# Four weight sums on GpSimd moved behind one transfer, in a transformer block on one core

## The chip, the core and the metric

The kernel runs on one core of a Trainium2 chip. The core has a matrix engine (TensorE, PE in the profile), three element-wise engines (VectorE or DVE, ScalarE or ACT, GpSimd or POOL), a synchronising engine that issues transfers (SyncE, SP), and sixteen DMA engines. Every engine takes its own instructions in the order in which they were written; between engines, semaphores order the work. The metric is device time in microseconds of one execution: 1111.73 us is the median of three runs of the kernel before (1110.59 to 1112.41).

## What is computed

A parallel block: a layer norm of x (2048 rows of 576), then x + attention + a feed-forward part, both taken from the same normed rows. The attention is local and dilated: 32 heads of 18, each position looks at 8 keys, 2 apart.

```python
def _A_ref(x, wqkv, wo):
    H = 32; Dh = D // H
    W, dil = 8, 2
    qkv = ... (x @ wqkv).reshape(B, S, 3, H, Dh) ...
    idx = pos[:, None] - off[None, :]            # off = arange(W) * dil
    logits = einsum("bhsd,bhswd->bhsw", q, k[idx]) * scale, masked where idx < 0
    o = einsum("bhsw,bhswd->bhsd", softmax(logits), v[idx])
    return o @ wo
def _B_ref(x, w1, w2):                           # w1: 576 x 4608, w2: 4608 x 576
    return maximum(x @ w1, 0) @ w2
x = A_x
xn = _layernorm(x)
return x + _A_ref(xn, A_wqkv, A_wo) + _B_ref(xn, B_w1, B_w2)
```

All data is float32.

## The kernel before

**Split numbers.** A float32 operand is split in two: a high part, which ScalarE writes as a rounded copy, and a low part, the rest, which VectorE or GpSimd gets by a subtraction (function `two`: L172 the copy, L176 the subtraction on VectorE, L174 the same on GpSimd where a call asks for `pooled`). A product is then three matmuls: high by high, high by low, low by high. Relu outputs are split in the same way: L793 is ScalarE's high part, L797 VectorE's low part.

**Tiling.** The 2048 rows are taken in two phases of 1024, each phase in four blocks of 256 columns after a transpose (`xT`, in SBUF). W1's 36 column tiles of 128 are taken first six by the plain way, and the other 30 in 15 pairs. A pair's product with two row blocks is a 2 by 2 block product over the first 512 of the 576 input features, done with seven products instead of eight (M1 to M7). For this the quarters A11, A12, A21, A22 of a pair of W1 are combined: S1 = A21 + A22, S2 = S1 - A11, S4 = A12 - S2, S3 = A11 - A21. `sw_load` brings the quarters into the staging tile `st` (DMAs from SyncE), `sw_mix(k)` makes one of the four combinations in `st` (L958, one GpSimd instruction on 128 x 256), and `sw_prep` splits quarters and combinations into the matmul operands in `ar` (L172 and L176). Each of these operands has one place, so a split for the next pair can only follow the last matmul that reads the old one.

**Groups and steps.** A pair p has an even group 2p (row blocks 0 and 1) and an odd group 2p + 1 (row blocks 2 and 3): 30 groups a phase. `group` runs a group in eight steps. A step is a half of the seven products (two runs of twelve matmuls on the two halves of TensorE's rows, banks `ph` and `pm`), followed by a half of the second weight's product for an earlier group (`po`, columns 0 to 255 or 256 to 575). The products share four accumulators: `a` and `q` (two `ph` banks, used in turn) and `f` and `r` (two `pm` banks, in turn). In step 2 ScalarE copies `a` into a new `q` bank, and in step 5 it copies `q` into a new `r` bank (`seed`, L1026). A bank is free again when its relu or its addition has read it. So the low part (L797) of the relu read from `pm` in step 4 frees the bank of the seed in step 5, which TensorE uses in step 7, and the L797 read from `ph` in step 6 frees the bank of `a` in step 1 of the next group. The relus of steps 1 and 2 read SBUF tiles `m` and `u` (L1035 completes them on VectorE).

**The output.** When the two column parts of a row block are complete in PSUM, ScalarE copies them into a buffer `ev` (L746, one copy of 512 and one of 640 numbers for each partition), and GpSimd issues a transfer that adds the buffer to the output in DRAM (L752). There are two such buffers, and two transfers a group: one issued in step 3, one in step 7.

**Who sets the order.** `plan_strassen` writes by `on(phase, group, step, "T" or "O", ...)` what is issued in which step: "T" behind the step's first products, "O" behind its second-weight half. Beside that a queue of attention work for VectorE (`bg`: L575 products of queries and keys, L578 their sums, L587 to L602 the softmax, L610 and L617 the weighted values, L626 and L633 transposes) is drained by `run_bg`, which at fixed points of each step issues as much as a running account of VectorE's time (`t["dve"]`, raised by every `dve(n)`) leaves room for. In three stretches of a phase steps also hold the splits of a slice of the attention weights (`wq`), and two groups later 26 or 28 matmuls for queries, keys and values (L142) behind four steps of a group.

A tensor's staging is also read by `w2_split` (the second weight; 256 and 320 columns, L172 and L176, on GpSimd L174 in even groups).

Of the kernel before, what the change touches and what calls it, by code (L numbers as in the profile page):

```python
# [70 lines left out]
def tile_body(ctx: ExitStack, tc: tile.TileContext, x, wqkv, wo, w1, w2, out):  # L71
# [1010 lines left out]
    def on(ph, g, i, z, f, *a):  # L1082
        evs[ph, g, i, z].append((f, a))
# [5 lines left out]
    def plan_strassen(ph):  # L1089
        for p in range(NP):  # L1090
            a = 2 * p
            f = NC0 * C + 2 * p
            if p:
                on(ph, a - 2, 4, "O", sw_load, ph, p)
                on(ph, a - 2, 8, "O", sw_mix, 0)
                on(ph, a - 1, 1, "O", sw_mix, 1)
                on(ph, a - 1, 2, "O", sw_mix, 2)
                on(ph, a - 1, 4, "O", sw_mix, 3)
                on(ph, a - 1, 4, "T", sw_prep, ph, p, "A11")
                on(ph, a - 1, 5, "O", sw_prep, ph, p, "S2")  # L1100
                on(ph, a - 1, 7, "T", sw_prep, ph, p, "S1", "A12")
                on(ph, a, 2, "O", sw_prep, ph, p, "S3", "S4")
                on(ph, a, 3, "T", sw_prep, ph, p, "A22", "rem")
                on(ph, a - 1, 5, "O", w2_load, ph, f)
                on(ph, a - 1, 6, "O", w2_load, ph, f + 1)
                on(ph, a, 6, "T", w2_split, ph, f, (0,), True)
                on(ph, a, 8, "T", w2_split, ph, f, (1,), True)
                on(ph, a + 1, 1, "O", w2_split, ph, f + 1, (0,))
                on(ph, a + 1, 3, "O", w2_split, ph, f + 1, (1,))
        for u in range(1, NU):  # L1110
            g = QKV_G[u]
            on(ph, g - 3, 4, "O", wq_load, ph, u)
            for kt, (d, i) in enumerate(((-2, 4), (-2, 7), (-1, 1), (-1, 4), (-1, 6))):
                on(ph, g + d, i, "O", wq_split, ph, u, kt)
            for tb in range(NTB):
                a, i = g + tb // 2, 3 + 4 * (tb % 2)
                ins[ph, a, i].append((qkv_half, (ph, u, tb, False, True)))
                ins[ph, a, i + 1].append((qkv_half, (ph, u, tb, True, True)))
            on(ph, g + 2, 1, "T", halos, ph, u)
            on(ph, g + 2, 1, "T", attention, ph, u)  # L1120
            on(ph, g + 2, 4, "T", attention_rest, ph, u)
        g = QKV_G[NU - 1] + 2
        on(ph, g, 1, "O", wo_first, ph)
        on(ph, g + 1, 5, "O", wo_split, ph, 0)
        on(ph, g + 3, 3, "O", wo_split, ph, 1)
        on(ph, g + 5, 3, "O", wo_split, ph, 2)
        on(ph, NG - 1, 5, "O", hold.__setitem__, ("xs", ph), True)
        if ph == 0:
            for i in range(2):
                on(ph, NG - 1, 4 + i, "O", xt_in, 1, i)  # L1130
            for i in range(2):
                on(ph, NG - 1, 8, "O" if i else "T", xt_parts, 1, i, 0)
                on(ph, NG - 1, 8, "O", xt_parts, 1, i, 1)
            on(ph, NG - 1, 5, "O", hold.__setitem__, ("go", 0), True)
            on(ph, NG - 2, 4, "O", w1_load, 1, 0)
            on(ph, NG - 1, 5, "O", w2_load, 1, 0)
            on(ph, NG - 1, 7, "O", w2_load, 1, 1)
            on(ph, NG - 1, 6, "O", w1_split, 1, 0, 0, True)
            on(ph, NG - 1, 8, "T", w1_split, 1, 0, 1)
# [291 lines left out]
    for ph in range(NPH):  # L1431
# [65 lines left out]
        late(b + 22, sw_prep, ph, 0, "S3", "S4")  # L1497
        late(b + 23, sw_prep, ph, 0, "A22", "rem")
        plan_strassen(ph)
    ot_plan(0)  # L1500
    ot_plan(1)
# [156 lines left out]
```

## Time and profile before

| what | value |
|---|---|
| median of the runs | 1111.73 us (1110.59 to 1112.41, three runs) |
| the profiled execution | 1111.74 us, span 1109.9 us |
| TensorE busy | 1098.9 us, 99% |
| VectorE busy | 849.0 us, 76% |
| ScalarE busy | 573.5 us, 52% |
| GpSimd busy | 357.9 us, 32% |
| sums of W1 quarters, L958 | 120 of 0.952 us |
| adding transfers, L752 | 128, on GpSimd's queue |

A row of the page's table of groups names the line, the engine, the operation, out<-in by the program's names, and how many; then busy us and mean ns of one, then the idle time of the engine before them and what ended it. A row of the waits reads: who waited for whom, us in total, times, longest. A row of the timeline has the start in us from the start of the span, the duration, engine, line, operation and tiles, and in brackets the idle time of the engine before it with what ended it. Operations that follow each other on an engine can overlap by some 0.07 us.

### The profile page before, as it was taken

The numbers are of one execution on the slowest core, as the hardware profiler recorded it, in microseconds if no ns is written. First come the engines' busy times: TensorE is split into PE (matmuls) and PEld (weight loads), VectorE is DVE, ScalarE is ACT, GpSimd is POOL, SyncE is SP. The second block draws the span as 40 slices with busy tenths as digits, with TensorE's granted clock in tenths as the row PEclk, the third lists the DMA queues.
The fourth block names the chain that finished last, engine by engine and source line by source line (L and its number), as shares of the span: only waits on it lengthen the run. The fifth ranks groups of instructions, "written<-read, shape, count | busy, mean of one in ns | idle before, by whom it ended". The sixth has DMA issues, their size and how long they took to land.

```text
span 1109.9 us, 37930 instructions
## 1 busy us (share of the span) xinstructions
PE 1098.9 (99%) x16410; PEld 1087.7 (98%) x16410; DVE 849.0 (76%) x1262; ACT 573.5 (52%) x1350; POOL 357.9 (32%) x377
## 2 busy tenths in 40 slices
PE   9999999999999999999999999999999999999998
PEld 8999999999999999999999999999999999999998
DVE  7676898898897889994326349987988978989751
ACT  5443564564455365666535346635635644566560
POOL 2313441343333234433211233313413333333421
PEclk9999999999999999999999999999999999999999
DMA  8369995696596598889958258749957965988896
GB/s 244 126 161 228 194 185 100 148 200 105 125 220 131 89 221 159 152 154 261 260 88 173 37 130 165 143 76 203 186 95 153 195 109 126 210 148 159 165 220 145
DMA packets 136598, 177.26 MB, mean 160 GB/s; under 512 B 27872, under 2 KB 83936, under 8 KB 136400
## 3 DMA queue, kind: packets, MB, share of 16 engines
q0 software_dynamic: 37632, 81.40, 47.0%
q1 hardware_dynamic: 98080, 92.55, 28.7%
q8 instruction: 129, 2.11, 0.7%
q10 hardware_dynamic: 720, 0.89, 0.2%
q14 instruction: 37, 0.30, 0.1%
HBM read 74.07 MB, written 96.22 MB: 153 GB/s over the span
## 4 chain that ended last, share of the span: by engine, by line
PE 86%; DMA 6%; DVE 3%; issue 2%; ACT 2%; SPq 1%; POOL 0%; DVEq 0%; ACTq 0%; POOLq 0%
PE po L163 28%; PE po L142 21%; PE ph L163 14%; PE pm L163 11%; PE pm L142 5%; PE ph L142 4%; DMA xT<-words 2%; PE ph L130 1%; PE po L130 1%; DMA out<-ev 1%; DMA st<-in_w 1%; DVE ar L797 1%; DVE ar L176 1%; DMA att<-od 1%; DMA od<-att 1%
## 5 line engine op out<-in xcount | busy, mean ns | idle before, releaser
L163 PE MATMUL po<-ar 64*128 64x320 f32 (+1 forms) x5760 | 455.7, 290 | 1.3 <-ACT pr L746 0.9
L163 PEld LDWEIGHTS po<-ar 64*128 64x128 f32 x5760 | 397.4, 184 | 3.2 <-ACT pr L746 1.3
L163 PE MATMUL ph<-xT,ar 64*128 64x256 f32 x2520 | 318.3, 275 | 1.1 <-DVE ar L797 0.5
L752 POOL DMA_DIRECT2D out<-ev x128 | 152.5, 1191 | 477.9 <-ACT ev L746 363.4
L163 PEld LDWEIGHTS ph<-xT,ar 64*128 64x128 f32 x2520 | 285.7, 185 | 2.4 <-ACT pm L1026 1.5
L163 PE MATMUL pm<-xS,ar 64*128 64x256 f32 x2160 | 258.0, 275 | 1.8 <-ACT u L1030 1.3
L746 ACT ACTIVATE ev<-po 128x512 f32<-128x512 f32 (+1 forms) x266 | 171.9, 652 | 137.5 <-PE po L163 74.5
L163 PEld LDWEIGHTS pm<-xS,ar 64*128 64x128 f32 x2160 | 236.1, 185 | 3.0 <-ACT u L1030 2.3
L176 DVE TENSOR_TENSOR ar<-st,ar 128x256 fp32r<-128x256 f32 (+3 forms) x236 | 157.3, 680 | 69.2 <-ACT ar L172 69.0
L172 ACT ACTIVATE ar<-st 128x256 fp32r<-128x256 f32 (+3 forms) x304 | 148.6, 503 | 3.1 <-DMA st<-in_w 1.9
L142 PE MATMUL po<-wq,xT 64*128 64x432 f32 x1296 | 133.8, 353 | 0.2 <-ACT ev L746 0.2
L142 PEld LDWEIGHTS po<-wq,xT 64*128 64x128 f32 x1296 | 120.4, 185 | 2.5 <-ACT ev L746 0.4
L174 POOL TENSOR_TENSOR ar<-st,ar 128x256 fp32r<-128x256 f32 (+1 forms) x68 | 74.5, 1098 | 132.8 <-ACT ar L172 129.9
L958 POOL TENSOR_TENSOR st<-st 128x256 f32<-128x256 f32 x120 | 113.7, 952 | 6.5 <-DMA st<-in_w 2.1
L163 PE MATMUL ph<-xS,ar 64*128 64x256 f32 x720 | 102.0, 275 | 0.1
L163 PEld LDWEIGHTS ph<-xS,ar 64*128 64x128 f32 x720 | 94.3, 185 | 0.4 <-ACT ph L1026 0.3
L610 DVE TENSOR_TENSOR pr<-att 128x1152 f32<-128x1152 f32 x64 | 88.1, 1392 | 0.4
L575 DVE TENSOR_TENSOR pr<-att 128x1152 f32<-128x1152 f32 x64 | 87.8, 1383 | 0.1
L578 DVE TENSOR_REDUCE att<-pr 128x64 f32<-128x1152 f32 x64 | 85.5, 1342 | 0.1
L142 PE MATMUL po<-ar 64*128 64x256 f32 (+1 forms) x984 | 72.7, 290 | 0.1
L617 DVE TENSOR_TENSOR pr<-pr 128x1152 f32<-128x1152 f32 x64 | 70.0, 1094 | 1.4
L797 DVE SCALAR_TENSOR_TENSOR ar<-ph,ar 128x256 fp32r<-128x256 f32 x96 | 39.0, 418 | 40.0 <-ACT ar L793 39.5
(120 smaller groups left out, 1365.1 us busy)
## 6 DMA issues: line engine op xcount, KB each, us to landing
out<-ev POOLq DMA_DIRECT2D x128, 576.0 KB, 7.3
st<-in_w SPq DMA_DIRECT2D x72, 288.0 KB, 5.6
st<-in_w SPq DMA_DIRECT2D x63, 256.0 KB, 3.6
att<-att SPq DMA_DIRECT2D x16, 441.0 KB, 4.5
att<-in_wqkv SPq DMA_DIRECT2D x28, 216.0 KB, 6.3
od<-att SPq DMA_DIRECT2D x32, 160.0 KB, 5.8
att<-in_x SPq DMA_DIRECT2D x14, 288.0 KB, 4.0
st<-in_w SPq DMA_DIRECT2D x60, 64.0 KB, 6.4
```

Source lines behind the costliest of these rows:

```text
L142: ins = nc.tensor.matmul(o, l[z], r[z], start=start, stop=stop)
L163: b.ins = nc.tensor.matmul(b.ap, l[part], r[part], start=start, stop=stop, skip_group_check=skip)
L172: nc.scalar.activation(hi, src, AF.Copy)
L174: nc.gpsimd.tensor_tensor(lo, src, f32(hi), op=ALU.subtract)
L176: nc.vector.tensor_tensor(lo, src, f32(hi), op=ALU.subtract)
L575: nc.vector.tensor_tensor(pr[i], q, window(k, i), op=ALU.mult)
L578: nc.vector.tensor_reduce(lg[:, i], pr.pop(i).rearrange(heads, d=Dh), axis=AX.X, op=ALU.add)
L610: nc.vector.tensor_tensor(pr[i].rearrange(heads, d=Dh), e, window(v, i).rearrange(heads, d=Dh), op=ALU.mult)
L617: nc.vector.tensor_tensor(o, z[:, :, 0:n], z[:, :, n : 2 * n], op=ALU.add)
L746: nc.scalar.activation(acc[:, :, cols], z[:, :, 0 : cols.stop - cols.start], AF.Copy)
L752: ADDED[ph, tb] = nc.gpsimd.dma_start(rows_of(ph, tb), acc, accum_op=ALU.add)
L958: nc.gpsimd.tensor_tensor(stg(o), stg(a), stg(b), op=op)
```

## The change

In each odd group but the last of a phase (28 in all) the four sums for the next pair stood in step 8 of the even group and steps 1, 2 and 4 of the odd one. Now all four are issued in step 4 of the odd group, and the split of S2 is issued in step 6 instead of step 5. Nothing is computed otherwise.

```diff
             if p:
                 on(ph, a - 2, 4, "O", sw_load, ph, p)
-                on(ph, a - 2, 8, "O", sw_mix, 0)
-                on(ph, a - 1, 1, "O", sw_mix, 1)
-                on(ph, a - 1, 2, "O", sw_mix, 2)
-                on(ph, a - 1, 4, "O", sw_mix, 3)
+                for k in range(4):
+                    on(ph, a - 1, 4, "O", sw_mix, k)
                 on(ph, a - 1, 4, "T", sw_prep, ph, p, "A11")
-                on(ph, a - 1, 5, "O", sw_prep, ph, p, "S2")
+                on(ph, a - 1, 6, "O", sw_prep, ph, p, "S2")
                 on(ph, a - 1, 7, "T", sw_prep, ph, p, "S1", "A12")
```

On GpSimd, between the two pooled splits of the second weight (`ar<-st_`, L174) of one even group and the transfer of step 7 of the odd group behind it (the group at 227 to 239 us of the profile), this stood before:

```order
L174 TENSOR_TENSOR ar<-st_4075,ar 128x256
L752 DMA out<-ev 128x2x576
L174 TENSOR_TENSOR ar<-st_4075,ar 128x320
L958 TENSOR_TENSOR st<-st 128x2x128 x3
L752 DMA out<-ev 128x2x576
L958 TENSOR_TENSOR st<-st 128x2x128
L752 DMA out<-ev 128x2x576 x2
```

and this stands there now:

```order
L174 TENSOR_TENSOR ar<-st_4073,ar 128x256
L752 DMA out<-ev 128x2x576
L174 TENSOR_TENSOR ar<-st_4073,ar 128x320
L752 DMA out<-ev 128x2x576
L958 TENSOR_TENSOR st<-st 128x2x128 x4
L752 DMA out<-ev 128x2x576 x2
```

Three sums moved past one transfer; the last two transfers are that of step 7 and the first of the next even group.

On VectorE, in steps 3 to 8 of the same odd group, from the split of the second weight's 320 columns to the additions into `u` and `m`, this stood before (the plain `ar<-st,ar 128x256` are the splits of A11 and S2, in this order, and `128x2x256` is that of S1 and A12):

```order
L176 TENSOR_TENSOR ar<-st_4110,ar 128x320
L797 SCALAR_TENSOR_TENSOR ar<-pm,ar 128x256
L176 TENSOR_TENSOR ar<-st,ar 128x256
L176 TENSOR_TENSOR wq<-att,wq 128x432
L575 TENSOR_TENSOR pr<-att 128x1152
L176 TENSOR_TENSOR ar<-st,ar 128x256
L797 SCALAR_TENSOR_TENSOR ar<-ph,ar 128x256
L578 TENSOR_REDUCE att<-pr 128x64
L176 TENSOR_TENSOR ar<-st,ar 128x2x256
```

and this stands there now:

```order
L176 TENSOR_TENSOR ar<-st_4110,ar 128x320
L797 SCALAR_TENSOR_TENSOR ar<-pm,ar 128x256
L176 TENSOR_TENSOR ar<-st,ar 128x256
L176 TENSOR_TENSOR wq<-att,wq 128x432
L575 TENSOR_TENSOR pr<-att 128x1152
L578 TENSOR_REDUCE att<-pr 128x64
L797 SCALAR_TENSOR_TENSOR ar<-ph,ar 128x256
L176 TENSOR_TENSOR ar<-st,ar 128x256
L176 TENSOR_TENSOR ar<-st,ar 128x2x256
```

The split of S2 went behind L797 from `ph`, and since it no longer counts in step 5's account, L578 went ahead of it. In 11 of the 28 odd groups an attention operation changes sides with L797 like this; in the other 17 only the split of S2 does. On ScalarE the copy for S2 went behind the keep of `m` (L1030), the relu's high part (L793) and an eviction (L746), in all 28. TensorE and SyncE keep their order.

## The prediction

> **What bounds the kernel now.** I read the page first, then the table of waits, then the timeline around single groups.
>
> ```profile
> span 1109.9 us, 37930 instructions
> PE 1098.9 (99%) x16410; PEld 1087.7 (98%) x16410; DVE 849.0 (76%) x1262; ACT 573.5 (52%) x1350; POOL 357.9 (32%) x377
> L958 POOL TENSOR_TENSOR st<-st 128x256 f32<-128x256 f32 x120 | 113.7, 952 | 6.5 <-DMA st<-in_w 2.1
> ```
>
> The profiled execution took 1111.74 us, 0.01 over the median of the three runs, so a sum against it is one against the median. TensorE (PE) is busy for all but 11 us, and much of that is at the start and the end. Nothing can be won but its few stalls, and every new stall adds its full length. The 120 sums on GpSimd (POOL), 0.952 us each, are in nobody's way directly: POOL is busy 32%. What they can do is hold up VectorE (DVE), on which banks of TensorE depend.
>
> ```profile
> PE ph L163 <- DVE ar L797: 0.5, 1, 0.5
> ACT pm L1026 <- DVE ar L797: 17.5, 18, 2.8
> ```
>
> Both rows have the same releaser: the low part of a relu (L797). Read from `pm` it frees the bank into which ACT then copies the seed (L1026) that TensorE needs in step 7; read from `ph` in step 6 it frees bank "a", which TensorE needs in step 1 of the next group. One odd group shows all of it (start, duration; VectorE, then GpSimd, ScalarE, TensorE):
>
> ```profile
> 229.04 1.69 DVE L797 SCALAR_TENSOR_TENSOR ar<-u,ar 128x256 fp32r<-128x256 f32 x1
> 230.65 0.95 DVE L797 SCALAR_TENSOR_TENSOR ar<-m,ar 128x256 fp32r<-128x256 f32 x1
> 233.68 1.03 DVE L176 TENSOR_TENSOR ar<-st,ar 128x320 fp32r<-128x320 f32 x1
> 234.62 0.41 DVE L797 SCALAR_TENSOR_TENSOR ar<-pm,ar 128x256 fp32r<-128x256 f32 x1
> 234.96 0.78 DVE L176 TENSOR_TENSOR ar<-st,ar 128x256 fp32r<-128x256 f32 x1
> 235.66 0.60 DVE L176 TENSOR_TENSOR wq<-att,wq 128x432 fp32r<-128x432 f32 x1
> 236.18 1.34 DVE L575 TENSOR_TENSOR pr<-att 128x1152 f32<-128x1152 f32 x1
> 237.45 0.41 DVE L176 TENSOR_TENSOR ar<-st,ar 128x256 fp32r<-128x256 f32 x1
> 237.79 0.41 DVE L797 SCALAR_TENSOR_TENSOR ar<-ph,ar 128x256 fp32r<-128x256 f32 x1
> 238.12 1.33 DVE L578 TENSOR_REDUCE att<-pr 128x64 f32<-128x1152 f32 x1
> 239.38 0.67 DVE L176 TENSOR_TENSOR ar<-st,ar 128x512 fp32r<-128x512 f32 x1
> ...
> 229.24 2.96 POOL L958 TENSOR_TENSOR st<-st 128x256 f32<-128x256 f32 x3
> 233.47 1.20 POOL L752 DMA_DIRECT2D out<-ev  x1 [1.27 <-ACT ev L746]
> 234.25 1.20 POOL L958 TENSOR_TENSOR st<-st 128x256 f32<-128x256 f32 x1
> 239.31 1.20 POOL L752 DMA_DIRECT2D out<-ev  x1 [3.86 <-ACT ev L746]
> ...
> 233.07 0.46 ACT L172 ACTIVATE ar<-st 128x320 fp32r<-128x320 f32 x1
> 236.47 0.61 ACT L746 ACTIVATE ev<-po 128x512 f32<-128x512 f32 x1
> 238.30 0.71 ACT L746 ACTIVATE ev<-po 128x640 f32<-128x640 f32 x1 [0.71 <-PE po L163]
> ...
> 237.23 1.04 PE L163 MATMUL po<-ar 64*128 64x320 f32 x12
> 238.10 0.28 PE L163 MATMUL pm<-xS,ar 64*128 64x256 f32 x1
> 238.79 0.84 PE L163 MATMUL po<-ar 64*128 64x256 f32 x12
> 239.47 0.73 PE L163 MATMUL ph<-xT,ar 64*128 64x256 f32 x10
> ```
>
> Three things are to be seen. First, the sums do not wait for the steps they stand in: three of them run back to back from 229.24, right behind the pooled split, and only the transfer of 233.47 holds the fourth. Second, while sums run, VectorE operations with two SBUF operands stretch: L797 from `m` takes 0.95 here, the same operation from a PSUM bank 0.41. I charge 0.54 for each VectorE operation that meets a sum. Reductions and operations that read PSUM keep their time. Third, the transfer waits for ScalarE's eviction, not for the sums, so standing ahead of them brings it nothing.
>
> The Trainium skill (SBUF — State Buffer, "Who interferes with whom") says that a VectorE instruction with two SBUF inputs contends with a GpSimd instruction that reads SBUF, that reductions never do, and that the one that issues first holds the port for its whole length. On who contends the rows agree. On the price they do not: by that sentence a blocked operation would lose the whole sum, 0.95 by the page of the profile instead of 0.54, and the 18 meetings counted below would cost 7.4 us more, 1122.4.
>
> **The change, part by part.** *Three sums leave steps 8, 1 and 2.* There VectorE gains about 3 x 0.54 = 1.6 us in each of 28 odd groups. Most of it is worth nothing: VectorE's next operation that counts is the 320-column split at 233.68, and that needs ScalarE's copy of 233.07, which follows an eviction and so TensorE. VectorE arrives early and waits. It pays only where VectorE reached that place late, and the trace shows where, since TensorE stalled behind it:
>
> ```profile
> 989.51 1.03 PE L163 MATMUL po<-ar 64*128 64x320 f32 x12
> 990.74 0.39 PE L163 MATMUL ph<-xT,ar 64*128 64x256 f32 x1 [0.20 <-ACT pm L1026]
> 994.51 0.39 PE L163 MATMUL ph<-xT,ar 64*128 64x256 f32 x2 [0.55 <-DVE ar L797]
> 1037.56 1.42 PE L163 MATMUL po<-ar 64*128 64x320 f32 x12
> 1038.79 0.37 ACT L1026 ACTIVATE pm<-ph 128x256 f32<-128x256 f32 x1 [2.79 <-DVE ar L797]
> 1039.21 0.39 PE L163 MATMUL ph<-xT,ar 64*128 64x256 f32 x1 [0.23 <-ACT pm L1026]
> 966.35 0.37 ACT L1026 ACTIVATE pm<-ph 128x256 f32<-128x256 f32 x1 [2.12 <-DVE ar L797]
> ```
>
> An undisturbed half of 320 columns gives way to the next step after 0.87 us (237.23 to 238.10). Here it took 1.23 (989.51) and 1.65 (1037.56): stalls of 0.36 and 0.78. The one of 994.51 is 0.55. After a stall the first pair of matmuls takes 0.39 instead of 0.28, 0.11 more. With 0.4 for the one behind the wait of 966.35 (an estimate, like the shortest of these) the stalls come to 0.36 + 0.78 + 0.55 + 0.4 + 4 x 0.11 = 2.5 us. I take all of it as won, since the delay that makes them is 1.6 us a group and the stalls are shorter.
>
> *Four sums now follow the transfer.* The first takes the place of the one that is there already (234.25, ending 235.45, with the split of A11 ending 0.29 behind it), so it costs nothing new. The second to fourth are new between the split of A11 and L797 from `ph`. Each meets one VectorE operation with two SBUF operands if there is one: `wq` split, L575, L610, L617.
>
> *The split of S2 goes to step 6.* It leaves the queue ahead of L797 from `ph`: 0.34 saved there (237.45 to 237.79). But the kernel's own account of VectorE time now has 0.4 us more room in step 5, and in 11 of the 28 odd groups this pulls an attention operation ahead of L797; in the group above it is L578, 1.26 (238.12 to 239.38). ScalarE copies S2 after its eviction, at 237.08; the second sum ends by about 235.45 + 0.29 + 0.60 = 236.3, so ScalarE does not wait. S2 is read in step 4 of the next group, more than five steps on. SP's queue keeps its order; the loads that it issues behind split buffers are not nearer to a release than before. The transfer of step 7 stands behind the fourth sum: with two meetings that ends near 239.2, the transfer goes at 239.31, so it is just free.
>
> So L797 from `ph` ends later by 0.54 x meetings + what was pulled ahead - 0.34. In the group above: 1.08 + 1.26 - 0.34 = 2.00. It ended at 238.20 and TensorE entered step 1 at 239.47, 1.27 of slack: a stall of 0.73. Other tight groups:
>
> ```profile
> 329.73 0.41 DVE L797 SCALAR_TENSOR_TENSOR ar<-ph,ar 128x256 fp32r<-128x256 f32 x1
> 331.07 0.39 PE L163 MATMUL ph<-xT,ar 64*128 64x256 f32 x4
> 493.24 0.42 DVE L797 SCALAR_TENSOR_TENSOR ar<-ph,ar 128x256 fp32r<-128x256 f32 x1
> 493.82 0.29 PE L163 MATMUL ph<-xT,ar 64*128 64x256 f32 x2
> 1017.08 0.42 DVE L797 SCALAR_TENSOR_TENSOR ar<-ph,ar 128x256 fp32r<-128x256 f32 x1
> 1018.00 0.39 PE L163 MATMUL ph<-xT,ar 64*128 64x256 f32 x4
> ```
>
> At 331.07 the same 2.00 meet 0.93 of slack: 1.07. At 493.82 three L617 lie between (three meetings, nothing pulled ahead): 1.62 - 0.34 = 1.28 against 0.16: 1.12. At 1018.00 the same 1.28 against 0.50: 0.78. The twin of the first group, 91 us before it, has the same order of work: 0.73. Three more (before 423, 470 and 694 us) come out at 0.2, 0.2 and 0.5 by the same sum. In the other 20 odd groups either a QKV half widens the steps, or one meeting less leaves the slack uneaten: 0. The eight add up to 0.73 + 1.07 + 1.12 + 0.78 + 0.73 + 0.9 = 5.3, with 8 x 0.11 behind them 6.2 us, over 18 meetings. The price of a meeting I know only from three sums in a row at 229 us. Its ends are 0, if VectorE's operation gets in first, and 0.95, if it waits out the sum; 0.54 is taken because those rows have the same engine, operand shapes and the same succession of sums.
>
> The sum is 1111.7 - 2.5 + 6.2 = 1115.4.
>
> **The rivals.** *Faster.* The meetings cost VectorE nothing, GpSimd waits instead: all of the 6.2 falls away and the 2.5 stay, 1109.2. The place is the stretch between the split of A11 and L797 from `ph`. For it speaks that VectorE's operations there are mostly long (L575, 1.34), so that a sum arrives while one is running. Against it: the sum of 234.25 was issued while VectorE was at work and still made the next split end behind it. It decides once a meeting costs under about 0.1. The Trainium skill's sentence on who issues first (SBUF — State Buffer, same section) names this case, with VectorE ahead. I give it 0.17.
>
> *No change that can be told* (within 0.2%, 2.2 us, about what a measurement of this kernel can tell). Meetings cost half, 0.27: the eight lateness values shrink to about 2.8 with what follows a stall, against 2.5 won, 1112. Speaks for it that long operations absorb part of a sum: 0.25.
>
> *Slower by another way.* Sums that wait out long VectorE operations end late, by 1.34 each at most, and then the transfer of step 7 is late and with it the buffer that ScalarE evicts into, or the copy of S2 holds ScalarE up. ScalarE has 0.71 idle before the next eviction (238.30) and 0.7 between sum and copy, so the lateness must pass 1.4 before TensorE feels it. If it did by 0.3 in 20 groups: 6 us on top, 1121. I give it 0.08.
>
> **How the numbers follow.** The forecast, late banks after step 6, has 0.50: 1115.4, of itself between 1114.0 (meetings of 0.4) and 1119.5 (0.8). Faster by over 0.2%: 0.17. Within: 0.25. Slower: 0.50 + 0.08 = 0.58. The range 1109.0 to 1120.0 leaves out the last rival, some of the 0.95 end, and a little below the faster rival.
>
> **What would show it.** Right: VectorE's L797 from `u` and `m` drop to 0.42 in steps 1 to 2; ScalarE's wait before L1026 on L797 shrinks from 17.5 us; TensorE's wait for `ph` on L797 grows from 0.5 to 4 to 6 us, at step 1 of even groups, near 148, 239, 331, 494 and 1018 us, while the stalls of 990 to 994 and 1039 us are gone; the four sums stand right behind the transfer, with L575, L610 and L617 stretched there. Wrong: no `ph` wait at those places (then the faster rival), ScalarE waiting for POOL at L172, or evictions waiting for transfers more often than now.

## The result, and the profile after

The changed kernel takes 1116.32 us (median of 6 runs, 1114.56 to 1118.19), the kernel before on the same chip 1111.70 (6 runs, 1110.59 to 1113.39). The ratio is 1.0036, 95% interval 1.0022 to 1.0050: slower by 4.6 us by the medians, 4.0 by the ratio. The profiled execution of the changed kernel took 1118.19 us, the longest of its six, so its trace shows some 2 us more than the median has.

The page, the groups by line, and the table of waits of the changed kernel:

```profile
span 1116.4 us, 37921 instructions
PE 1102.2 (99%) x16410; PEld 1088.3 (97%) x16410; DVE 831.8 (75%) x1262; ACT 572.7 (51%) x1350; POOL 379.5 (34%) x377
L958 POOL TENSOR_TENSOR st<-st 128x256 f32<-128x256 f32 x120 | 126.2, 1065 | 6.7 <-DMA st<-in_w 2.1
...
DVE ar L176 <- ACT ar L172: 93.9, 45, 15.9
ACT ev L746 <- DMA out<-ev: 18.9, 21, 2.1
ACT pm L1026 <- DVE ar L797: 5.4, 7, 1.1
PEld ph L163 <- DVE ar L797: 5.2, 9, 1.2
PE ph L163 <- DVE ar L797: 3.1, 6, 1.0
ACT ar L172 <- POOL st L958: 0.6, 1, 0.6
```

VectorE (DVE) has 17 us less to do than before (849.0 to 831.8), and the kernel is slower all the same. It does the same 1262 instructions, so it lost less time to GpSimd in all, but what it loses now lies ahead of a bank that TensorE needs. ScalarE's wait before the seed fell from 17.5 us to 5.4, TensorE's for `ph` on L797 rose from 0.5 to 3.1 (5.2 more stand at its weight loads, 0.7 before). The group that the prediction showed, in the changed kernel's timeline (start, duration; VectorE, GpSimd, ScalarE, TensorE):

```profile
230.70 1.00 DVE L797 SCALAR_TENSOR_TENSOR ar<-u,ar 128x256 fp32r<-128x256 f32 x1
231.62 0.42 DVE L797 SCALAR_TENSOR_TENSOR ar<-m,ar 128x256 fp32r<-128x256 f32 x1
235.22 0.49 DVE L176 TENSOR_TENSOR ar<-st,ar 128x320 fp32r<-128x320 f32 x1 [1.58 <-ACT ar L172]
235.97 1.43 DVE L176 TENSOR_TENSOR ar<-st,ar 128x256 fp32r<-128x256 f32 x1
237.32 1.14 DVE L176 TENSOR_TENSOR wq<-att,wq 128x432 fp32r<-128x432 f32 x1
238.39 1.89 DVE L575 TENSOR_TENSOR pr<-att 128x1152 f32<-128x1152 f32 x1
240.20 1.34 DVE L578 TENSOR_REDUCE att<-pr 128x64 f32<-128x1152 f32 x1
241.46 0.41 DVE L797 SCALAR_TENSOR_TENSOR ar<-ph,ar 128x256 fp32r<-128x256 f32 x1
...
230.07 1.33 POOL L174 TENSOR_TENSOR ar<-st,ar 128x320 fp32r<-128x320 f32 x1
235.13 1.20 POOL L752 DMA_DIRECT2D out<-ev  x1 [3.73 <-ACT ev L746]
235.91 1.20 POOL L958 TENSOR_TENSOR st<-st 128x256 f32<-128x256 f32 x1
237.19 0.81 POOL L958 TENSOR_TENSOR st<-st 128x256 f32<-128x256 f32 x1
238.07 2.80 POOL L958 TENSOR_TENSOR st<-st 128x256 f32<-128x256 f32 x2
241.61 1.20 POOL L752 DMA_DIRECT2D out<-ev  x1 [0.73 <-ACT ev L746]
...
239.79 0.93 ACT L172 ACTIVATE ar<-st 128x256 fp32r<-128x256 f32 x2
...
240.45 0.84 PE L163 MATMUL po<-ar 64*128 64x256 f32 x12
241.93 0.74 PE L163 MATMUL ph<-xT,ar 64*128 64x256 f32 x8 [0.63 <-DVE ar L797]
```

The four sums stand right behind the transfer and meet three VectorE operations in a row: the split of A11 (1.43), the split of `wq` (1.14), L575 (1.89). L578 comes ahead of L797, which ends at 241.87. By then TensorE runs 1.66 us later than before, so that is 240.21 on the clock of before, where it ended at 238.20: 2.01 later. TensorE enters step 1 0.80 late.

Both kernels have the same 16,410 matmuls in the same order, so the start of each can be set against its start before; where the difference jumps, time was lost or won. Ten jumps of a second trace of the changed kernel (below) are set beside those of the first, each without the 0.11 that follows a stall. All differences are against the first trace of the kernel before:

| place (us in the kernel before) | predicted | first trace | second trace |
|---|---|---|---|
| 148, 239 | 0.73 each | 0.79, 0.80 | 0.79, 0.79 |
| 331 | 1.07 | 1.15 | 0.45 |
| 423, 470 | 0.2 each | 0.29, 0.31 | 0.29, 0.30 |
| 494 | 1.12 | 0.12 | 0.17 |
| 694 | 0.5 | 0.40 | 0.39 |
| 1018 | 0.78 | 0.61 | 0.62 |
| 786, 878 | 0 | 0.26, 0.33 | 0.26, 0.24 |
| together | 5.3 | 5.1 | 4.3 |
| with 0.11 behind each | 6.2 | 6.2 | 5.4 |
| stalls of 966 to 1039 | -2.5 | -2.5 | -2.5 |
| net | 3.7 | 3.7 | 2.9 |

The first trace is 6.6 us behind the trace of before at its last matmul, so 2.9 us were lost elsewhere: about 1.6 where one half of the positions passes into the other (516 to 550 us), 0.4 in the first 35 us, the rest mostly at evictions and copies of ScalarE.

### The profile page after: what moved, and what is told of

It reads as the page before. It is cut to its first block, busy times and chain, and to the rows that moved or that the text cites. A ratio compares the mean times of both kernels' runs of the same rounds, so it can differ in the third digit from the quotient of the medians.

```text
span 1116.4 us, 37921 instructions
## 1 busy us (share of the span) xinstructions
PE 1102.2 (99%) x16410; PEld 1088.3 (97%) x16410; DVE 831.8 (75%) x1262; ACT 572.7 (51%) x1350; POOL 379.5 (34%) x377
## 4 chain that ended last, share of the span: by engine, by line
PE 88%; DMA 4%; DVE 4%; issue 1%; ACT 1%; SPq 0%; DVEq 0%; POOL 0%; ACTq 0%; POOLq 0%
PE po L163 29%; PE po L142 22%; PE ph L163 14%; PE pm L163 11%; PE pm L142 5%; PE ph L142 4%; DMA out<-ev 2%; PE ph L130 1%; PE po L130 1%; DVE ar L176 1%; DMA st<-in_w 1%; DVE pr L617 1%; DVE ar L797 1%; DMA od<-att 1%; DMA att<-wo 1%
## 5 line engine op out<-in xcount | busy, mean ns | idle before, releaser
L746 ACT ACTIVATE ev<-po 128x512 f32<-128x512 f32 (+1 forms) x266 | 171.8, 651 | 130.0 <-PE po L163 62.7
L176 DVE TENSOR_TENSOR ar<-st,ar 128x256 fp32r<-128x256 f32 (+3 forms) x236 | 147.0, 644 | 94.2 <-ACT ar L172 93.9
L172 ACT ACTIVATE ar<-st 128x256 fp32r<-128x256 f32 (+3 forms) x304 | 145.7, 504 | 4.5 <-DMA st<-in_w 2.9
L958 POOL TENSOR_TENSOR st<-st 128x256 f32<-128x256 f32 x120 | 126.2, 1065 | 6.7 <-DMA st<-in_w 2.1
L174 POOL TENSOR_TENSOR ar<-st,ar 128x256 fp32r<-128x256 f32 (+1 forms) x68 | 74.9, 1103 | 130.7 <-ACT ar L172 126.3
L575 DVE TENSOR_TENSOR pr<-att 128x1152 f32<-128x1152 f32 x64 | 92.4, 1457 | 0.1
L610 DVE TENSOR_TENSOR pr<-att 128x1152 f32<-128x1152 f32 x64 | 89.5, 1417 | 0.4
L578 DVE TENSOR_REDUCE att<-pr 128x64 f32<-128x1152 f32 x64 | 85.4, 1344 | 0.2
L797 DVE SCALAR_TENSOR_TENSOR ar<-ph,ar 128x256 fp32r<-128x256 f32 x96 | 39.1, 418 | 39.4 <-ACT ar L793 38.9
```

What stands on the lines that cost most here:

```text
L172: nc.scalar.activation(hi, src, AF.Copy)
L174: nc.gpsimd.tensor_tensor(lo, src, f32(hi), op=ALU.subtract)
L176: nc.vector.tensor_tensor(lo, src, f32(hi), op=ALU.subtract)
L575: nc.vector.tensor_tensor(pr[i], q, window(k, i), op=ALU.mult)
L578: nc.vector.tensor_reduce(lg[:, i], pr.pop(i).rearrange(heads, d=Dh), axis=AX.X, op=ALU.add)
L610: nc.vector.tensor_tensor(pr[i].rearrange(heads, d=Dh), e, window(v, i).rearrange(heads, d=Dh), op=ALU.mult)
```

## Experiments

Each time is the median of 5 to 12 runs, except for the two second traces, and each ratio is against runs of the kernel before taken beside them. The medians of the kernel before were 1112.66 us for the first four kernels, 1112.36 for the next two, and 1112.20 for the last three, on another chip. That is 0.5 to 1.0 above the 1111.7 from which the expectations were counted, so the ratios are the surer measure.

**The split alone.** The kernel before, with one line changed:

```diff
-                on(ph, a - 1, 5, "O", sw_prep, ph, p, "S2")
+                on(ph, a - 1, 6, "O", sw_prep, ph, p, "S2")
```

> The kernel before with only the split of S2 moved to step 6; the four sums stand where they stood. Theory (a late bank "a" needs the pulled-ahead attention operation and the meetings together): L797 from ph ends later by 1.26 - 0.34 = 0.92 in the groups where an operation is pulled ahead, against slacks of 1.27 (148 and 239 us) and 0.93 (331 us), so TensorE's wait for ph on L797 stays under 1.0 us in all and the time at 1111.5 to 1112.3. Rival (the pulled-ahead operation does the harm alone): that wait is 3 us or more, 1114.5 or above.

1111.48 us, ratio 0.9984 (0.9974 to 0.9993). The shown group in its timeline:

```profile
237.49 1.34 DVE L578 TENSOR_REDUCE att<-pr 128x64 f32<-128x1152 f32 x1
238.75 0.41 DVE L797 SCALAR_TENSOR_TENSOR ar<-ph,ar 128x256 fp32r<-128x256 f32 x1
239.51 0.73 PE L163 MATMUL ph<-xT,ar 64*128 64x256 f32 x10
```

L578 is pulled ahead, L797 ends at 239.16 instead of 238.20 (0.96, expected 0.92), and TensorE enters step 1 at 239.51 as before (239.47): the slack holds it. So the pulled-ahead operation alone does hardly any harm (0.3 us at 878, 0.2 at 331). The kernel is even a little faster than the one before: the interval lies wholly below 1, though the gain is less than the 0.2% named in the prediction. Where it comes from, the trace does not tell.

**The sums alone.** The changed kernel, with the split of S2 put back in step 5:

```diff
-                on(ph, a - 1, 6, "O", sw_prep, ph, p, "S2")
+                on(ph, a - 1, 5, "O", sw_prep, ph, p, "S2")
```

> The changed kernel with the split of S2 put back in step 5; only the sums are moved. Theory: two meetings cost 1.08, nothing is pulled ahead, the split of S2 (0.34) is ahead of L797 again; 148 and 239 us keep their slack of 1.27, 331 loses about 0.15, 470, 494 and 1018 lose 0.4 to 1.0 each; with the 2.5 won that is 1111.5 to 1113.0. ScalarE's copy of S2 waits for the second sum, about 0.9 us in each odd group, some 20 us in all, and TensorE feels none of it. Rival (ScalarE's wait is passed on, which is why the split had to go a step later): 0.3 us or more in most groups, 1116 or above.

1120.84 us, ratio 1.0071 (1.0057 to 1.0086). The theory missed, and the time is that of the rival; its mechanism is not. Table of waits, and the shown group in the timeline:

```profile
ACT ar L172 <- POOL st L958: 30.3, 19, 2.8
PEld ph L163 <- DVE ar L797: 8.5, 14, 1.2
PE ph L163 <- DVE ar L797: 5.6, 11, 1.0
...
238.16 0.42 ACT L172 ACTIVATE ar<-st 128x256 fp32r<-128x256 f32 x1 [1.50 <-POOL st L958]
238.52 1.89 DVE L575 TENSOR_TENSOR pr<-att 128x1152 f32<-128x1152 f32 x1
240.33 0.95 DVE L176 TENSOR_TENSOR ar<-st,ar 128x256 fp32r<-128x256 f32 x1
241.21 0.41 DVE L797 SCALAR_TENSOR_TENSOR ar<-ph,ar 128x256 fp32r<-128x256 f32 x1
241.68 0.97 PE L163 MATMUL ph<-xT,ar 64*128 64x256 f32 x12 [0.25 <-DVE ar L797]
```

ScalarE's copy of S2 stands ahead of its parts of the relu and waits 1.50 us for the second sum. But the copy is done (238.58) while VectorE is still in L575, and VectorE goes on without a gap. What makes L797 late is the split of S2 itself: it meets the fourth sum (0.95 for 0.41) and is ahead of L797. The same holds at 148, 216, 307, 399, 423 and 470 us; these seven stalls come to 5.1 us. ScalarE's lateness can be in the other losses, some 2.5 us at its copies and evictions; that was not separated. TensorE stalls at more places than in the changed kernel: 0.61 at 216, 307 and 399 us, where that one has nothing, 1.17 at 423 and 1.19 at 470. So the step that the split was moved is worth 4.5 us once the sums are moved (1120.84 to 1116.32; by the two ratios 3.9), and without it moving the sums costs twice as much.

**One sum only.** The changed kernel, with:

```diff
-                for k in range(4):
+                for k in range(1):
```

> The changed kernel with the second, third and fourth sum of every odd group left out, so that part of the computation is missing; the first sum and all splits stay, in the order of the changed kernel. Theory (the meetings make the lateness): the pulled-ahead operation alone, 0.92 late, fits the slack; no ph wait on L797 above 0.5 us in all, the stalls of 966 to 1039 us stay gone, 1109.0 to 1110.0. Rival (the loss has another cause, the order or the transfers): 1113 or above.

1109.30 us, ratio 0.9967 (0.9956 to 0.9979), as the theory had it. Its timeline in the shown group:

```profile
234.86 1.44 DVE L176 TENSOR_TENSOR ar<-st,ar 128x256 fp32r<-128x256 f32 x1
236.22 0.60 DVE L176 TENSOR_TENSOR wq<-att,wq 128x432 fp32r<-128x432 f32 x1
236.74 1.34 DVE L575 TENSOR_TENSOR pr<-att 128x1152 f32<-128x1152 f32 x1
239.27 0.41 DVE L797 SCALAR_TENSOR_TENSOR ar<-ph,ar 128x256 fp32r<-128x256 f32 x1
240.03 0.84 PE L163 MATMUL ph<-xT,ar 64*128 64x256 f32 x12
```

The split of A11 still meets the first sum (1.44 for 0.41); the split of `wq` and the attention operations run at their free durations. No wait of TensorE for `ph` on L797 is left in the table of waits, although L578 is still pulled ahead. The second to fourth sum are what makes L797 late enough to stall TensorE.

**The order of the attention operations kept.** The changed kernel, with the account of VectorE time charged in step 5 and given back in step 6:

```diff
+                on(ph, a - 1, 5, "O", dve, 256)
                 on(ph, a - 1, 6, "O", sw_prep, ph, p, "S2")
+                on(ph, a - 1, 6, "O", dve, -556)
```

> The changed kernel, but its account of VectorE time still charges the split of S2 in step 5, so no attention operation is pulled ahead of L797 from ph; sums and split stand as in the changed kernel. Theory: the lateness is 0.54 x meetings - 0.34; the stalls at 148, 239, 331, 423, 694, 786 and 878 us go (4.8 us in the trace of the changed kernel, with what follows them), those at 470 and 1018 stay: 1111.0 to 1112.0. Rival (the meetings alone make the lateness): the stalls stay and the time is 1114.5 or above.

1113.95 us, ratio 1.0009 (0.9998 to 1.0021). The time lies between the two expectations; the stalls fell as the theory had it, nearly:

```profile
237.49 1.89 DVE L575 TENSOR_TENSOR pr<-att 128x1152 f32<-128x1152 f32 x1
239.30 0.41 DVE L797 SCALAR_TENSOR_TENSOR ar<-ph,ar 128x256 fp32r<-128x256 f32 x1
240.23 0.84 PE L163 MATMUL ph<-xT,ar 64*128 64x256 f32 x12
1020.76 0.97 PE L163 MATMUL ph<-xT,ar 64*128 64x256 f32 x12 [0.45 <-DVE ar L797]
```

L575 meets its sum as in the changed kernel (1.89), but L797 follows it at once, and TensorE has no wait. The stalls of 148, 239, 331, 694, 786 and 878 us are gone, those of 470 (0.30) and 1018 (0.62) stand; that of 423 (0.28) stayed against what was expected, since in that group no attention operation had been pulled ahead. So meetings and pulled-ahead operation are both needed for the large stalls, and the pulled-ahead one is worth 2.4 us of the 4.6 (1116.32 less 1113.95; by the two ratios 3.0 of 4.0). The median is 2 us above the expected range. One of them is in the kernel before, which took 1112.66 here; for the rest, this trace too loses 1.4 us between 516 and 550 us, where TensorE waits for ScalarE and not for L797.

**The sums in a place where VectorE waits.** The kernel before, with the first sum waiting for the low part of the relu from `m`, and the second and third behind it; then the same with the fourth sum ahead of the transfer too:

```diff
-            nc.vector.scalar_tensor_tensor(lo, src, 0.0, f32(hi), op0=ALU.max, op1=ALU.subtract)
+            LAST[0] = nc.vector.scalar_tensor_tensor(lo, src, 0.0, f32(hi), op0=ALU.max, op1=ALU.subtract)
...
-        nc.gpsimd.tensor_tensor(stg(o), stg(a), stg(b), op=op)
+        z = nc.gpsimd.tensor_tensor(stg(o), stg(a), stg(b), op=op); k or tc.add_manual_dep(z.ins, LAST[0].ins.name, SYNC, reason="m")
...
-                on(ph, a - 2, 8, "O", sw_mix, 0)
+                on(ph, a - 1, 1, "O", sw_mix, 0)
```

and, for the second kernel, besides:

```diff
-                on(ph, a - 1, 4, "O", sw_mix, 3)
+                on(ph, a - 1, 2, "O", sw_mix, 3)
```

> The kernel before with one more wait: the first sum of an odd group waits for the low part of the relu from m, so that the first three sums run in the stretch in which VectorE itself waits for ScalarE, ahead of the 320-column split; the fourth sum and the split of S2 stand as before. Theory (sums cost only where they meet VectorE on its way to something): in the changed kernel's group near 230 us L797 from m ends at 232.04 and the transfer goes at 235.13, 3.1 us for three sums of 0.8 each, so they meet little, L797 from u and m run at 0.42, the stalls of 966 to 1039 us (2.5) go and no new ones come: 1109.0 to 1110.5. Rival (the sums then meet the 320-column split and the split of A11, or hold up the transfer): 1112 or above.

> The kernel of the run before this one with the fourth sum too ahead of the transfer, behind the third. Theory: the four take about 3.2 us and fit the 3.1 us up to the transfer nearly, the split of A11 meets no sum any more (0.41 instead of 0.78), the stall of 494 us (0.5) goes as well: 1108.5 to 1110.0. Rival: the fourth sum makes the transfer late and the eviction that waits for its buffer with it, 1112 or above.

1111.31 us, ratio 0.9997 (0.9987 to 1.0008), and 1113.52 us, ratio 1.0012 (1.0000 to 1.0024). In both the stalls of 966 to 1039 us are gone (2.3 and 2.7 us). The stall of 494 us, which the expectations of these and of later runs count on, does not exist: TensorE enters there without a wait in the kernel before (493.82 in the prediction's rows), and the 0.5 in its table of waits is the stall of 994.51.

The first kernel gave most of its 2.3 us back in pieces, 1.2 us of them at evictions of ScalarE (894 and 951 us). The second gave back more, mostly at evictions. TensorE near 951 us in the first kernel's timeline, then ScalarE and TensorE in the second's:

```profile
952.60 0.97 PE L163 MATMUL po<-ar 64*128 64x256 f32 x12 [0.55 <-ACT ev L746]
```

```profile
954.04 0.60 ACT L746 ACTIVATE ev<-po 128x512 f32<-128x512 f32 x1 [3.92 <-DMA out<-ev]
954.69 0.97 PE L163 MATMUL po<-ar 64*128 64x256 f32 x12 [1.90 <-ACT ev L746]
```

The eviction waits for an earlier transfer out of its buffer. In the kernel before it waits there too (1.49 us), just short of a stall. In the second kernel, four such places (221, 405, 859 and 951 us) cost 5.0 us. It has the least VectorE time of all complete kernels here (811.9 us) and is not faster for it.

**A second trace** of each of the two kernels, one execution each.

> The kernel before once more, for a second trace of it. If the stretch from 516 to 550 us (where one half of the positions passes into the other, and the changed kernel's trace lost 1.6 us that no step of the change explains) differs from one execution to the next, this trace differs from the first there by 0.5 us or more; if it is a matter of the kernel, it agrees within 0.2.

> The changed kernel once more, for a second trace. If what it lost at 516 to 550 us is a matter of the execution, that loss is 1.0 us or less here; if it comes from the change, 1.6 again. The stalls of TensorE behind L797 at 148, 239, 331, 423, 470, 694, 878 and 1018 us should be there again with the same lengths within 0.2.

The kernel before took 1114.85 us this time. At 516 to 550 us its trace wins 0.3 us on the first, which decides neither way. Near 123 us it loses 4.0 us: GpSimd's sums there wait 7.4 us for their weights (2.1 in the first trace), and ScalarE and TensorE wait behind them. GpSimd and TensorE in its timeline:

```profile
123.33 4.40 POOL L958 TENSOR_TENSOR st<-st 128x256 f32<-128x256 f32 x4 [7.38 <-DMA st<-in_w]
123.15 0.38 PE L163 MATMUL ph<-xT,ar 64*128 64x256 f32 x1 [1.50 <-ACT pm L1026]
126.83 0.38 PE L163 MATMUL pm<-xT,ar 64*128 64x256 f32 x1 [1.40 <-ACT m L1030]
```

This trace also shows something that the prediction's sum needs: it has the stalls of 990, 994 and 1037 us, but not the one of 966 us. ScalarE's seed, which waited 2.12 us for L797 in the first trace (966.35), waits 1.02 here, and TensorE does not stall:

```profile
968.67 0.37 ACT L1026 ACTIVATE pm<-ph 128x256 f32<-128x256 f32 x1 [1.02 <-DVE ar L797]
```

In the first trace an eviction 4 us earlier had waited 1.70 us for a transfer, here 0.97. In none of the other traces, those with the sums in their old places included, does TensorE stall at that step. So 0.5 of the 2.5 us was one execution's, and 2.0 are the change's.

The changed kernel took 1117.00 us. Its stalls behind L797 are those of the table, all but one within 0.1; 331 us has 0.45 for 1.15. From 516 to 550 us it loses 1.0, the bound that was named for a matter of the execution, and it has an eviction at 710 us that waits for a transfer and costs 1.15, which the first trace has not. So single executions differ by 1 to 4 us at transfers. That the stretch at 516 us is slower through the change can't be told: of the other kernels, the split alone and the kept order lose 1.4 us each there and the sums alone 0.7, the one with one sum wins 0.5, the five others range from a loss of 0.4 to a gain of 1.2, and no part of the change goes with that.

**Split and waiting sums put together**: the split alone with the account kept as in the fourth experiment; the waiting sums with the split moved; and both with the account kept.

> The kernel before with only the split of S2 moved to step 6, and the account of VectorE time still charging it in step 5, so that no attention operation is pulled ahead. Theory: L797 from ph ends 0.34 earlier in every odd group and nothing comes in its place; the stall at 494 us (0.5 and 0.1 behind it) goes, those of 966 to 1039 us stay (their delay comes from the sums): 1110.5 to 1111.8, 0.5 to 1.0 under before. Rival (what the run with the split alone gained came from the pulled-ahead operations): as before, 1112 to 1112.8.

> The first sum waits for the low part of the relu from m, as in the earlier run, and the split of S2 stands in step 6, with the attention operations that this pulls ahead. Theory: the stalls of 966 to 1039 us and of 494 us go, the one meeting that is left (the fourth sum) and the pulled-ahead operation (0.92 late) fit the slack; the evictions wait for transfers as in any run: 1109.5 to 1111.0. Rival (the waiting sums cost what they save, by transfers that go later): 1111.5 or above.

> As the run before this one, with the account of VectorE time still charging the split in step 5: L797 from ph 0.34 earlier, nothing pulled ahead, no sum ahead of L797 from u and m. Theory: the least lateness of all these orders, 1109.0 to 1110.8. Rival (transfers): 1111.5 or above.

1111.63 us, ratio 0.9994 (0.9984 to 1.0003); 1113.13 us, ratio 1.0005 (0.9994 to 1.0016); 1111.60 us, ratio 0.9989 (0.9980 to 0.9999). The first agrees with its theory in the median, but its interval takes in 1, and it had no stall at 494 us to win. The two with waiting sums hit their rivals in time. Between 966 and 1039 us both win 2.6 us, and they lose 2.0 and 1.1 us at 951 us, again an eviction. That is not all: the second kernel stalls 1.0 us in all behind L797 at 148, 239, 331, 786 and 878 us, so the pulled-ahead operation did not fit the slack, and the third stalls once, at 470 us (0.85), behind an L610 that took 2.94 while sums ran. The row is from the third kernel's timeline:

```profile
471.15 0.97 PE L163 MATMUL ph<-xT,ar 64*128 64x256 f32 x12 [0.64 <-DVE ar L797]
```

The split alone has the lowest ratio of the complete kernels, 0.16% under the kernel before, but its interval overlaps that of the last kernel (0.11% under).

## Why the prediction was right, and where its terms were off

- *The kind of loss* (a late L797 from `ph` holds bank "a") is right. With the second to fourth sum left out all ten stalls go, and the kernel is 3.4 us faster than the one before beside it (1109.30 and 1112.66); the faster rival had been given 2.5. Of 5.3 us predicted behind L797 the traces show 5.1 and 4.3. Part of this agreement is luck: the eight places that were named give 4.5 and 3.8, since 494 us lacks 1.0, and two places put at 0 add 0.6 and 0.5.
- *The gain of 2.5* is 2.0. The traces show 2.5 at the four places named, but the stall of 966 us was one execution's (see the second trace of the kernel before). With 2.0 the prediction's sum would have been 1115.9.
- *"The first \[sum\] ... costs nothing new"* is right by an offset. It took 0.54 from the 320-column split and 0.37 from the split of A11; now it takes 1.02 from A11's alone, which comes 0.65 earlier on the clock of before. Hence 2.01 for 2.00 at 239 us.
- *The price of 0.54* holds for the splits of `wq` (1.14 for 0.60) and L575 (1.89 for 1.34). That a blocked operation waits until the other is done, as the Trainium skill says (SBUF — State Buffer, "Who interferes with whom"), I set aside too readily. What an operation loses in the shown group is about what is left of the sum that is running when it comes, less some 0.1: 1.02 of 1.14 for A11's split, which begins 0.06 behind the first sum; 0.54 of 0.68 for that of `wq`, which begins 0.13 into a sum of 0.81; 0.55 of 0.66 for L575, 0.32 into the third (0.98). The fourth in turn waits out L575. The 0.54 of the 320-column split in the kernel before does not fit this: that split ended 0.74 ahead of the recorded end of its sum.
- *The sums at other prices* don't come out. Redone for the eight places, a meeting of 0.4 gives 1112.8 and not 1114.0, one of 0.8 gives 1120.1 and not 1119.5, one of 0.95 gives 1122.8 and not 1122.4, and at 0.27 the stalls come to 1.7 and not 2.8. So the forecast hung on the price more than its band said.
- *494 us, 1.12 for 0.12*: the term that was furthest off. The sum counted three new meetings and no old one. In the kernel before, A11's split of this very group takes 1.66, so it had already lost 1.25 to the fourth sum; in the changed kernel it takes 0.70. That 0.96 is to be set against the three meetings. The row stood in the trace and was not read.
- *"In the other 20 odd groups ... 0"*: 786 and 878 us cost 0.26 and 0.33 in the first trace. Both have a pulled-ahead L578 and one meeting, 1.46 by the prediction's own sum, against slacks of 1.13 and 0.77: that would have given 0.33 and 0.69, had it been worked out.
- *The split's step counted as a loss only*: 2.4 us for the pulled-ahead operation is right in kind, but the step does more than take 0.34 out of the queue. In step 5 the split meets the fourth sum ahead of L797, and the time is 1120.84. ScalarE's wait for the second sum, of which the prediction says that it does not come, is 30.3 us in all with the split in step 5, but in the groups that stall most VectorE does not wait for it. In the changed kernel ScalarE waits once, 0.6 us, near 497 us.
- *TensorE's wait for `ph` on L797, 4 to 6 us*: in the row that the prediction quoted it is 3.1 and 2.2, since part of the wait stands at the weight loads (5.2 and 4.6). The matmuls' starts give the 5.1 and 4.3 of the table.
- *L797 from `u` at 0.42*: it takes 1.00, since it overlaps the pooled split of 230.07; from `m` it is 0.42 as said.
- *Late transfers* (0.08): evictions wait 18.9 and 16.2 us for transfers, 21 times in each trace; in the two traces of the kernel before it is 14.5 and 9.6 us, 15 and 14 times. The prediction had named this as a sign of being wrong. One stall of 1.15 in the second trace is of that kind. It may be part of why the median is 0.9 us above the forecast, but with the sums in their old places other kernels wait 8.8 and 17.5, so how much of it is the change's stays open.

## What to carry to other kernels

Two engines' contention is not priced by how much of it there is, but by what stands behind it: here VectorE lost 17 us less to GpSimd and the kernel took 4.6 us more. Before moving work to a "free" place, look which bank or buffer the next operations on the disturbed engine release, and with how much slack, and take off what that place already loses. A step that is moved along with it may be what keeps the rest from being worse, so try each part alone.

## What the runs showed of the hardware that was not expected

Which of two operations gets in first turns on tenths of a microsecond, and not simply on the recorded start. The split of A11 and the sums behind the transfer, in the timeline of the changed kernel's first trace at 331 us:

```profile
328.49 1.78 DVE L176 TENSOR_TENSOR ar<-st,ar 128x256 fp32r<-128x256 f32 x1
328.78 4.98 POOL L958 TENSOR_TENSOR st<-st 128x256 f32<-128x256 f32 x4
```

in its second trace:

```profile
328.29 0.70 DVE L176 TENSOR_TENSOR ar<-st,ar 128x256 fp32r<-128x256 f32 x1
328.57 4.79 POOL L958 TENSOR_TENSOR st<-st 128x256 f32<-128x256 f32 x4
```

and in the kernel before, ahead of 494 us:

```profile
488.78 1.66 DVE L176 TENSOR_TENSOR ar<-st,ar 128x256 fp32r<-128x256 f32 x1
488.94 1.20 POOL L958 TENSOR_TENSOR st<-st 128x256 f32<-128x256 f32 x1
```

A split that begins 0.05 behind the sum took 1.43 or 1.44 (0.41 free) in all 18 groups of the changed kernel's trace that have it so. One that begins 0.16 ahead still waited (1.66). One that begins 0.28 or 0.29 ahead took about 0.7 in nine of the ten cases of five traces, and 1.78 in the tenth: with this one case goes the difference of 0.70 us between the two traces at 331 us. The Trainium skill (SBUF — State Buffer, "Who interferes with whom") says that who issues first holds the port and the other waits. The rows agree that one waits for most of what is left of the other, but the earlier start in the profile is not a sure sign of who that is. Part of this may lie in the records: a sum right behind a transfer is recorded with 1.20 us, against some 0.8 elsewhere, and its record starts 0.42 us before that of the transfer's issue ends (235.91 and 236.33 in the changed kernel's shown group).
